# A planned five-queue attention and feed-forward kernel: transfers planned 1.3 times as long, new due times, first batch loaded in larger pieces

## The chip, the cores and the metric

The kernel runs on one core of a Trainium2 chip. The metric is the device time of one execution in microseconds (us), the median of several. Times of the kernel before drift by 1 to 3 us from chip to chip, so comparisons between runs go by the ratio to the kernel before, timed in the same rounds on the same chip.

## The reference, cut to what matters

```python
# batch 8, heads 12, sequence 448, head size 64; model width 768, hidden width 2048
q_n, k_n = rmsnorm(q, g_q), rmsnorm(k, g_k)
attn = softmax(q_n @ k_n.T / sqrt(64))
x = (attn @ v), heads side by side          # 8 * 448 rows of 768
h = x @ w_in                                # first layer
out = (h * erf(softplus(h))) @ w_out        # second layer
```

## The kernel before

The kernel records every operation with an engine, a planned cost, a due time and the tiles that it reads and writes. A small planner then simulates the five queues (P TensorE, V VectorE, A ScalarE, G GpSimd, S SyncE) and writes the operations out in the order in which its simulation started them. On the chip each queue runs in exactly that order. The planner is greedy: an engine that is free takes, of the operations that the simulation holds ready, the one with the earliest due time. When a transfer lands in the simulation decides which work counts as ready.

```python
    SEM = 0.06
    ...
        def dma_next():
            heads = [r[0] for r in rings.values() if r]
            ...
            cycle = sum(o.work[1] for o, _ in heads) / 16       # us per packet, 16 engines
            return dma_now + min(left[0] for _, left in heads) * cycle, cycle
```

`work` is the number of packets and the engine time of one; a landing comes `lat` after the last packet. Loads and due times, cut:

```python
    def add_unit(n, a_key):             # q and k of four heads of a later batch
        tg = (12 + 13 * u if b == 1 else BATCH * (b - 1) + 15 * u)
        ...  add("S", 0.59, tg - 15, dma_start(...), lat=1.7, work=(512, 0.038))
        ...  add("G", ..., tg, ... squares ...);  add("V", ..., tg, ... tensor_reduce ...)
    def add_norm(b, p):                 # scale k on GpSimd, q on VectorE: due 54 b + 9 p - 20
    def add_transposes(...):            # DMA transposes from SyncE: due t0 - 14
    def add_pe_transposes(p):           # batch 0: transposes on TensorE, k copied out by V, q by A
    def add_normalise(b, p, a_key):     # xT = o * r on VectorE: due -1e3 + t0
    def add_act_block(b, after):        # softplus, erf on ScalarE; g = h * sp on VectorE: due -1e4 + b
    def add_w_in(c, sync): ...          # 4 pieces of 1.5 MB f32, each waiting for the one before
    def add_w_out(c, sync): ...         # 8 pieces, all after pair 5 of batch 1
```

Batch 0 is loaded pair by pair (12 main transfers of 192 KB).

## Time and profile before

| | before |
|---|---|
| median of three | 518.85 us (518.63 to 518.98) |
| span of the profiled run | 517.3 us |
| busy: TensorE, ScalarE, VectorE, GpSimd | 465.3, 383.5, 329.6, 255.8 us |

TensorE's busy time overstates its use: it also contains idle products (put in to keep the clock up) and products at half clock. So this text counts products instead. The *lost time* of a stretch is its length less 0.190 us for each useful product of 448 columns and less 0.1625 us for each of 384 that the trace has in it, the rates of the gapless closing stream (18.24 us for 96, 36.41 us for 224). The small transposes of batch 0 and the idle products count as lost. A product that runs across a cut counts on both sides, so short stretches can sum to some 0.7 us less than one long stretch.

Two waits off TensorE matter later, from the view of waits of the kernel before (who waited, for whom: total us, times, longest; in profile lines PE is TensorE, PEld its weight load, DVE VectorE, ACT ScalarE, POOL GpSimd, SP SyncE, and a q marks the issue of a transfer):

```profile
POOL sq L284 <- DMA rq<-in_k_dram: 31.9, 13, 5.8
DVE qn L250 <- DMA qT<-qn: 25.3, 9, 9.3
```

GpSimd stands 31.9 us at squares whose data haven't landed, VectorE 25.3 us at scalings whose buffer a transposing transfer still reads. Both queues run in order, so all work behind them stands too.

### The profile page before, as it was taken

Reading aid. Unit: us, or ns where it says so; the run is one execution under the profiler, and the core shown is the slowest. Engines: PE = TensorE matmul, PEld = TensorE weight load, DVE = VectorE, ACT = ScalarE, POOL = GpSimd, SP = SyncE. Lnnn points to the kernel's source line nnn. Section 1 sums busy time; section 2 is a strip of 40 time slices with the busy share of each in tenths; the row PEclk is TensorE's granted clock in tenths of the full one; section 3 lists DMA queues with packets and bytes.
Section 4 is the critical chain, followed back from the end, with each engine's and each line's share of the span. In section 5 each row is a group of like instructions: output and inputs, shape, how many; then the busy total and the mean of one; then the engine's idle time right before and its main releaser. Section 6 shows DMA issues by size and latency. Waiting matters only on the chain.

```text
span 517.3 us, 7578 instructions
## 1 busy us (share of the span) xinstructions
PE 465.3 (90%) x2516; PEld 245.4 (47%) x2516; DVE 329.6 (64%) x493; ACT 383.5 (74%) x508; POOL 255.8 (49%) x411
## 2 busy tenths in 40 slices
PE   7867489958989898999889999999989999999997
PEld 3433235523445444554445444554545555555664
DVE  5866278668766886658654795649763873367721
ACT  3766648796868987799666987898877987995700
POOL 5559488784597257733674257743764050000000
PEclk9899979988999999999998999999999999999999
DMA  7976987895997056951886136962774041110122
GB/s 174 250 146 114 193 182 176 159 222 78 186 226 215 30 125 103 227 157 30 157 188 148 60 88 140 187 182 59 158 159 121 30 72 34 47 61 1 62 76 77
DMA packets 133415, 65.98 MB, mean 128 GB/s; under 512 B 84224, under 2 KB 133376, under 8 KB 133376
## 3 DMA queue, kind: packets, MB, share of 16 engines
q1 hardware_dynamic: 126320, 58.42, 49.7%
q0 software_dynamic: 5440, 6.29, 8.2%
q10 hardware_dynamic: 1616, 0.79, 0.6%
q8 instruction: 20, 0.33, 0.3%
q14 instruction: 19, 0.16, 0.1%
HBM read 45.61 MB, written 11.01 MB: 109 GB/s over the span
## 4 chain that ended last, share of the span: by engine, by line
PE 49%; DMA 16%; POOL 12%; DVE 10%; issue 6%; ACT 4%; SPq 2%; POOLq 0%; DVEq 0%
PE f L557 18%; PE f L508 16%; PE o L454 9%; PE s L432 6%; POOL sq L284 5%; DMA qT<-qn 5%; DMA rq<-in_k_dram 4%; DVE h L495 2%; DMA w_in_sb<-in_moe_w_in_dram 2%; DVE g L537 2%; DVE qn L250 2%; ACT e L438 2%; DMA sp<-in_k_dram 2%; POOL kn L258 1%; DVE xT L468 1%
## 5 line engine op out<-in xcount | busy, mean ns | idle before, releaser
L508 PE MATMUL f<-xT,w_in_sb 128*128 128x448 bf16 x768 | 165.3, 357 | 14.4 <-DVE h L495 12.1
L438 ACT ACTIVATE e<-s 128x896 bf16<-128x896 f32 x144 | 129.4, 913 | 19.6 <-PE s L432 10.9
L557 PE MATMUL f<-w_out_sb,g 128*128 128x384 bf16 x768 | 132.7, 327 | 1.2 <-DMA w_out_sb<-in_moe_w_out_dram 1.2
L508 PEld LDWEIGHTS <-w_in_sb 128*128 128x128 bf16 x768 | 75.8, 99 | 88.2 <-issue 21.7
L557 PEld LDWEIGHTS <-g 128*128 128x128 bf16 x768 | 75.4, 98 | 55.6 <-issue 4.6
L432 PE MATMUL s<-qT,kp 128*128 128x448 bf16 x336 | 96.1, 358 | 5.4 <-ACT e L438 2.4
L454 PE MATMUL o<-e,vm 128*128 128x448 bf16 x288 | 73.1, 359 | 21.0 <-DVE xT L468 16.5
L495 DVE COPY h<-f 128x448 f32<-128x448 f32 x109 | 67.3, 620 | 35.9 <-PE f L508 34.9
L495 DVE COPY ob<-f 128x384 f32<-128x384 f32 x53 | 29.5, 556 | 72.6 <-PE f L557 66.2
L258 POOL TENSOR_TENSOR kn<-rk,st 128x384 bf16<-128x384 f32 x42 | 38.7, 922 | 71.5 <-ACT st L291 62.9
L287 DVE TENSOR_REDUCE st<-sq 128x16 f32<-128x1024 f32 (+1 forms) x42 | 45.5, 1084 | 29.0 <-POOL sq L284 28.6
L537 DVE TENSOR_TENSOR g<-h,sp 128x768 bf16<-128x768 f32 x64 | 62.4, 1002 | 0.0
L462 ACT ACTIVATE r<-o 64x448 f32<-64x448 f32 x48 | 26.0, 541 | 45.5 <-PE o L454 45.1
L284 POOL TENSOR_TENSOR sq<-rq 128x1024 f32<-128x1024 f32 x21 | 40.1, 1911 | 38.7 <-DMA rq<-in_k_dram 31.9
L250 DVE TENSOR_TENSOR qn<-rq,st 128x512 bf16<-128x512 f32 x42 | 42.1, 1013 | 26.8 <-DMA qT<-qn 25.3
L522 ACT ACTIVATE sp<-h 128x1792 f32<-128x1792 f32 x32 | 52.0, 1687 | 5.4 <-DVE h L495 5.3
L454 PEld LDWEIGHTS <-vm 128*128 128x128 bf16 x288 | 28.2, 98 | 51.8 <-issue 24.9
L526 ACT ACTIVATE sp<-sp 128x1792 f32<-128x1792 f32 x32 | 52.6, 1690 | 0.1
L432 PEld LDWEIGHTS <-kp 128*128 128x128 bf16 x336 | 33.0, 99 | 36.8 <-issue 7.1
L315 POOL TENSOR_TENSOR qT<-qT,gcomb 128x448 bf16<-128x448 bf16 x42 | 41.4, 987 | 9.9 <-DMA qT<-qn 7.8
L468 DVE TENSOR_TENSOR xT<-o,r 64x448 bf16<-64x448 f32 x48 | 29.3, 611 | 10.0 <-ACT r L466 9.0
L408 POOL CAST vx<-vs 64x64 bf16<-64x64 f32 x96 | 25.9, 271 | 19.6 <-DMA vs<-in_v_dram 10.8
(64 smaller groups left out, 436.2 us busy)
## 6 DMA issues: line engine op xcount, KB each, us to landing
vl<-in_v_dram SPq DMA_DIRECT2D x48, 192.0 KB, 2.9
out_dram<-ob SPq DMA_DIRECT2D x48, 192.0 KB, 1.9
rq<-in_q_dram SPq DMA_DIRECT2D x21, 384.0 KB, 3.9
rk<-in_k_dram SPq DMA_DIRECT2D x21, 384.0 KB, 4.7
w_in_sb<-in_moe_w_in_dram POOLq DMA_DIRECT2D x4, 768.0 KB, 9.3
w_out_sb<-in_moe_w_out_dram POOLq DMA_DIRECT2D x8, 384.0 KB, 5.4
vs<-in_v_dram SPq DMA_DIRECT2D x16, 96.0 KB, 3.9
out_dram<-ob SPq DMA_DIRECT2D x16, 96.0 KB, 2.2
```

Of the source, the lines that this page charges most:

```text
L250: add(eng, cost, due, lambda: e.tensor_tensor(qn.rearrange("p g h d -> p h g d"), raw, w[:, :, :, None].to_broadcast((P, 2, 4, D)), op=ALU ...
L284: add("G", 0.0019 * ng * D, tg, lambda raw=raw, ng=ng: nc.gpsimd.tensor_tensor(sq[:, :ng], raw.rearrange("p h j d -> p (h j) d"), raw.rear ...
L287: add("V", 0.14 + ng * D / 960, tg, lambda ss=ss, g0=g0, ng=ng: nc.vector.tensor_reduce(ss[:, g0 : g0 + ng], sq[:, :ng], axis=AX.X, op=ALU ...
L432: add("P", 0.1887, t0 + s - 1, lambda st=st, i=i, c0=c0: nc.tensor.matmul(st[:, i, :S], kk[:, c0 : c0 + P], qq, start=True, stop=True), re ...
L438: add("A", 0.918, t0 + s, lambda e=e, st=st: nc.scalar.activation(e, st[:, :, :S], func=FN.Exp), reads=[("s", sl, 0), ("s", sl, 1), a_key] ...
L454: add("P", 0.1887, t0 + s + 0.5, lambda s=s, half=half, lhs=lhs, rhs=rhs: nc.tensor.matmul(o_ps[half][:, :S], lhs, rhs, start=(s == 0), st ...
L495: nc.vector.tensor_copy(dst, src)
L508: add("P", 0.1887, 1e4 + BATCH * (b + 1) + f, lambda f=f, kt=kt, fp=fp: nc.tensor.matmul(fp[:, :S], w_in_sb[:, kt, f * P : (f + 1) * P], x ...
L522: last = add("A", 1.665 + (1.283 if c == 0 else 0), -1e3, lambda c=c, ci=ci: nc.scalar.activation(sps[c], hs[ci], func=FN.Softplus), reads ...
L526: add("A", 1.665 + (1.283 if c == 0 else 0), -1e3, lambda c=c: nc.scalar.activation(sps[c], sps[c], func=FN.Erf), writes=[("sp", c, 1), "t ...
L537: add("V", 0.95, -1e4 + b, lambda h=h, s=s, gm=gm, a=a: nc.vector.tensor_tensor(gm[:, a], h[:, a, 0:384], s[:, a, 0:384], op=ALU.mult), re ...
L557: add("P", 0.1617, 1e4 + BATCH * (b + 2.5) + ti, lambda src=src, col=col, nt=nt, js=js, fp=fp: nc.tensor.matmul(fp[:, :JS], src[nt // 4][: ...
```

## The change

The intent is a plan that is nearer to what the chip does. The diff, cut to its core:

```diff
-    SEM = 0.06
+    SEM = 0.05
-            cycle = sum(o.work[1] for o, _ in heads) / 16
+            cycle = 1.3 * sum(o.work[1] for o, _ in heads) / 16
# due times (some 30 in all; the ones that the argument touches)
-        tg = (12 + 13 * u if b == 1 else BATCH * (b - 1) + 15 * u)
+        tg = 29.7 + 14.65 * u if b == 1 else BATCH * (b - 1) + 15.43 + 19.0 * u
-        add_norm_k("G", (0.86, 0.25), tg, ...            # tg = 54 b + 9 p - 20
+        add_norm_k("G", (0.86, 0.25), tg - 35.25, ...    # tg = 54 b + 9 p
-        add("G", 0.5, t0 - 5, ... vm cast
+        add("G", 0.5, t0 - 8.95, ... vm cast
-        add("V", 0.617, -1e3 + t0, ... xT
+        add("V", 0.617, -100 * 1e3 + t0, ... xT
-                    add("S", 0.59, BATCH * (b + 3), ... store of out
+                    add("S", 0.59, BATCH * (b + 0.68), ... store of out
# engines of batch 0
-        add("V", 1.08, t0 - 22, ... tensor_copy(kps[kp], tk)
+        add("A", {"V": 1.08, "A": 0.92}, t0 - 27.47, ... evac_to(mk, kps[kp], tk)
-        add("A", 0.545, t0 - 22, ... activation(qTs[m], tq, Copy, scale=gcomb)
+        add("VA", {"V": 0.617, "A": 0.545}, t0 - 27.47, gained, ...
# first loads: pairs 0 | 1 | 2 and 3 | 4 and 5
-        for p in range(NP):
-            main("S", p, 1, k)
-            main("A" if p < 3 else "S", p, 0, q)
+        for g, hh in enumerate((slice(0, 2), slice(2, 4), slice(4, 8), slice(8, H))):
+            for i, (e, src) in enumerate((("A" if g < 2 else "S", q), ("S", k))):
+                load(...)
# pacing of the weights
-    load, ends = add_w_in(0, [first]), []
+    load, ends = plan.writer[("q0", 1)], []
-            if b == 0 and p < NC - 1:
-                load = add_w_in(p + 1, [load, ends[-1]])
-            if b == 1 and p == NP - 1:          # all eight pieces of w_out
+            if b == 0 and 0 <= p - W_IN < NC:   # W_IN = 0
+                load = add_w_in(p - W_IN, [load, ends[-1]])
+            if b == 1 and p >= W_OUT:           # W_OUT = 3: pieces spread over pairs 3, 4, 5
```

The arithmetic of the kernel doesn't change. What changes is the order of the queues, the engine of twelve copies, the size of the first loads (eight of the twelve are joined into four), and the places of the weight loads.

## The prediction

> **What bounds the kernel now.** I first asked what the end of the run hangs on. The chain that ended last closes with two pieces:
>
> ```profile
> 459.32 18.24 PE f L508 x96
> 477.56 36.41 PE f L557 x224
> ```
>
> The columns are start, duration and what ran. From 459 us to the end TensorE streams without a gap. The two rows also give the rate of a full stream: 18.24 / 96 = 0.190 us for a product of 448 columns and 36.41 / 224 = 0.163 us for one of 384. The run therefore ends when TensorE has worked off a fixed amount, and only TensorE time lost earlier can be won back. The page counts 768 + 336 + 288 + 96 = 1488 useful products of 448 columns (first layer, scores, attention outputs) and 768 + 128 = 896 of 384 (second layer). That is 1488 x 0.190 + 896 x 0.163 = 283 + 146 = 429 us out of 517; some 88 us are lost.
>
> Next I read where, in the busy times of stretches that I chose by the digits of the page's slices (columns: stretch, its length, then PE, PEld, DVE, ACT, POOL busy with instruction counts, granted clock, DMA share, GB/s):
>
> ```profile
> 0.00:70.00 70.00, 47.47 (x249) 22.73 (x250) 39.54 (x76) 40.25 (x72) 43.57 (x93) 0.93 0.86 175
> 70.00:100.00 30.00, 29.21 (x152) 14.72 (x151) 24.36 (x35) 23.90 (x41) 26.77 (x43) 0.99 0.77 177
> 100.00:120.00 20.00, 12.30 (x55) 5.65 (x54) 12.98 (x18) 19.14 (x17) 12.99 (x17) 0.88 0.97 171
> 120.00:390.00 270.00, 252.63 (x1357) 133.05 (x1355) 188.64 (x265) 215.80 (x292) 160.10 (x236) 0.99 0.65 140
> 390.00:517.30 127.30, 123.65 (x709) 69.24 (x709) 64.07 (x102) 84.37 (x90) 12.41 (x25) 1.00 0.21 56
> ```
>
> The same stretches asked for single lines give the useful products: 117 (10 + 51 + 56; the other 132 are 66 idle products that keep the clock up and 66 small transposes) up to 70 us, so 70 - 22 = 48 us lost; 152 from 70 to 100 us, 1 us lost; 55 from 100 to 120 us, 20 - 10.5 = 9.5 us lost; 884 wide and 473 narrow from 120 to 390 us, 270 - 245 = 25 us lost; and 4 us in the rest, most of it the drain after the last product. So the first 120 us hold 57 of the 88 us. The first 70 us can't be emptied: batch 0 must pass attention before the first layer has rows to work on.
>
> What holds TensorE up in these stretches, from the view of waits (who waited, for whom, total, times, longest):
>
> ```profile
> PE o L454 <- DVE xT L468: 16.5, 13, 5.5
> PE f L508 <- DVE h L495: 12.1, 12, 3.9
> PE o L454 <- POOL vm L403: 4.1, 2, 2.9
> PE f L331 <- POOL g L258: 2.5, 1, 2.5
> ```
>
> None of these operations is slow; they stand behind others in the fixed order of their engine. Two places in the timeline show it (start, duration, engine, line, operation; in brackets the idle time before it):
>
> ```profile
> 26.61 1.89 POOL L284 TENSOR_TENSOR sq<-rq 128x1024 f32<-128x1024 f32 x1
> ...
> 30.21 0.96 POOL L403 CAST vm<-vl 128x384 bf16<-128x384 f32 x2
> ...
> 30.79 1.31 PE L454 MATMUL o<-e,vm 128*128 128x448 bf16 x6 [2.86 <-POOL vm L403]
> ```
>
> Here the squares of batch 1 and a weight load that waits 0.82 us for its predecessor stand ahead of the value cast that batch 0 needs at once.
>
> ```profile
> 55.68 5.61 SPq L309 DMA_TRANSPOSE kp<-kn  x1
> ...
> 61.39 1.21 SPq L312 DMA_TRANSPOSE qT<-qn  x1
> ...
> 64.77 1.09 DVE L250 TENSOR_TENSOR qn<-rq,st 128x512 bf16<-128x512 f32 x1 [9.26 <-DMA qT<-qn]
> 65.89 0.62 DVE L468 TENSOR_TENSOR xT<-o,r 64x448 bf16<-64x448 f32 x1
> ...
> 66.56 0.91 PE L454 MATMUL o<-e,vm 128*128 128x448 bf16 x2 [5.53 <-DVE xT L468]
> ```
>
> VectorE stands 9.26 us at a query scaling of batch 1, whose buffer a transposing transfer has yet to read; the transfer stands in SyncE's queue behind another. The normalisation that frees the PSUM of batch 0 stands behind the scaling, and TensorE behind that. At 100 to 120 us it is the same: the square waited 2.8 us for its load, the reduction on VectorE 3.5 us for the square, and the first layer 3.9 and 3.1 us for evacuations on VectorE.
>
> **What the Trainium skill says.** "DMA: Bandwidth & Descriptors", section "Issuing engines are not separate DMA queues", says that transfers from all issuing engines run on the same 16 DMA engines and interleave, so several issuers save only issue time. The trace agrees: the share is 0.98 and 1.01 at 10 to 30 us, with sync, scalar and gpsimd issues in flight together. So fewer, larger first loads save issues (0.37 to 0.84 us each) but hardly bytes per us. The same page's "Bandwidth" gives 341 GB/s for 1 MB; here the best of the 40 slices has 250. "TensorE: Matmul & The Clock Gate", Part 1, says that an idle array falls to half clock for some 3.4 us. The trace agrees: after the gap at 61 to 66.6 us weight loads come 0.37 us apart, not 0.19, and the clock in 100 to 120 us is 0.88, so a long gap costs more than itself. "GPSIMD Engine Reference", section "Specifications", has GpSimd's SBUF interface shared with VectorE's two-input operations; L250 takes 0.69 us when undisturbed and 1.01 in the mean here.
>
> **The change, part by part.** It adds and removes almost no work; it re-sorts five queues.
>
> *Transfers 1.3 times as long.* The plan's unit of 896 KB has 512 x 0.038 x 2 + 256 x 0.018 x 2 = 48.1, over 16 engines 3.0 us plus 1.7, which is about 305 GB/s. The trace lands the large loads in 3.9 and 4.7 us and moves 175 GB/s in the busy first part. So the old plan puts users of a load ahead of work that is really ready sooner. A factor of 1.3 (235 GB/s) is nearer. It answers the waits on queries and squares above.
>
> *Due times.* Preparation of the next batch's unit goes from 12 + 13u to 29.7 + 14.65u for batch 1 and 15 to 23 later for others, so the square at 26.6 us should no longer pass ahead of the cast at 30.2 us. The cast's own due goes from -5 to -8.95. Normalisation (-1e5) now outranks the products of the activation block (-1e4), which before outranked it. Stores of the output become due 2.3 batches earlier; VectorE waited 6.2 us for those buffers.
>
> By stage, taking half of what the waits name where the order is the cause. Up to 70 us: casts 4.1 + transposes 2.5 + normalisation 7.2 (of the 16.5, the share before 75 us) = 13.8 us, plus some 12 products at the slow clock, 12 x 0.18 = 2 us; half of 16 is 8 us. From 100 to 120 us: 9.5 us lost, and I take 4 back, since ScalarE is busy 19.1 of 20 us there with the softplus and erf block and stays so. From 120 to 390 us: normalisation 9.3 and stores' knock-on; I take 3.
>
> *First batch.* Main loads go from 12 to 8, 4 x 0.47 = 2 us of issue saved on SyncE; the load of v's last rows (vs), for which the first cast waits 8.6 us, was issued at 12.7 us. Bytes ahead of it are the same: 1 us won. But pairs 2 and 3 now wait for one common load.
>
> *What it costs.* Six key evacuations move from VectorE (0.62 us each) to ScalarE (0.92, estimated from the exponent of the same size, 0.913) and six query evacuations (0.63) may leave it: +5.5 - 3.8 = +1.7 us on ScalarE, which is on the way in batch 0. First-layer weights start a pair later (17.8 us to about 20.5, after pair 0); four transfers of 9.3 us, one after another, then end near 63 us rather than 61. Together I charge 3 us.
>
> Sum: -8 - 4 - 3 - 1 + 3 = -13 us, which is 506.
>
> **Rivals.** (1) The first 70 us are bound by bytes: DMA share 0.86 there and 1.01 at the worst. Then the re-sorted order only moves the wait from casts to loads, and only the later 7 us are won: 512, within 2%. Against it speaks that the share falls to 0.58 at 40 to 50 us, in the midst of the stall. (2) The late preparation makes batch 1 start late: its squares and scalings fall into 60 to 100 us, where GpSimd is already busy 26.8 of 30 us, and TensorE waits for kp and qT. With second-layer weights now starting at pair 3 of batch 1 instead of pair 5, GpSimd also gets up to five issues of 0.76 us there. That gives 515 to 525. (3) The order fits so much better that stage 1 nears ScalarE's bound (37.2 us of work in the 56 us from 10 to 66): 12 us won there and 8 later, 498.
>
> **Range and chances.** The lines are 508.5 (2% faster) and 529. The three rivals spread 498 to 520; I take 506, and 494 to 517 for eight in ten. As the dues look fitted to a model and not to round numbers, and the wait they address is seen in the trace, faster has 0.61; same 0.35; slower 0.04.
>
> **What would show it.** Right: in the new profile the first first-layer stream starts before 65 us instead of 70.9; the 9.26 and 5.53 us waits are gone; the wait of attention outputs for the normalisation falls from 16.5 to under 9 us; the clock at 60 to 70 us is near 1; the last stream has the same length and starts some 13 us sooner. Wrong: kp or qT waits of TensorE at 60 to 100 us (rival 2), or a DMA share near 1 right through 10 to 60 us with the first-layer stream still near 70 (rival 1). The sum fails if new head-of-line waits appear after 120 us, since there the dues changed everywhere.

## The result, and the profile after

The changed kernel took 493.61 us in the median (492.1 to 494.1, 4 runs), beside 518.91 us (518.63 to 520.23) for the kernel before: ratio 0.9503, 95% interval 0.9476 to 0.953. The prediction was 506 us with a range of 494 to 517; the gain of some 25 us is twice the predicted one and just outside the range.

The end of the chain of waits of the changed kernel (start, duration, what):

```profile
432.09 18.16 PE f L515 x96
450.25 36.41 PE f L564 x224
```

The closing stream is as long as before (18.16 and 36.41 against 18.24 and 36.41 us) and starts 27 us sooner. TensorE's rate didn't change; time lost before 432 us was won back. (Line numbers moved: L515 is the first layer, L564 the second, L445 scores, L467 attention outputs.) The busy times of the same stretches (columns as in the prediction):

```profile
0.00:70.00 70.00, 56.55 (x300) 28.05 (x301) 47.86 (x86) 53.70 (x90) 50.71 (x106) 0.95 1.00 192
70.00:100.00 30.00, 28.81 (x150) 14.37 (x149) 22.31 (x30) 25.10 (x35) 25.75 (x38) 1.00 1.17 223
100.00:120.00 20.00, 13.23 (x60) 6.19 (x59) 14.72 (x20) 17.12 (x21) 11.99 (x16) 0.83 0.73 140
120.00:390.00 270.00, 263.38 (x1452) 141.67 (x1451) 195.86 (x278) 236.12 (x309) 161.10 (x242) 1.00 0.64 140
390.00:490.30 100.30, 96.65 (x561) 54.57 (x558) 47.28 (x76) 57.75 (x62) 5.05 (x13) 1.00 0.19 51
```

Asked for single lines, these stretches hold 168, 150, 60, 908 and 209 useful wide products, and 544 and 352 narrow ones in the last two. That gives:

| stretch | lost before, us | lost after, us | won | predicted |
|---|---|---|---|---|
| 0 to 70 | 47.8 | 38.1 | 9.7 | 6 (8 + 1 - 3) |
| 70 to 100 | 1.1 | 1.5 | -0.4 | 0 |
| 100 to 120 | 9.6 | 8.6 | 1.0 | 4 |
| 120 to 390 | 25.2 | 9.1 | 16.1 | 3 |
| 390 to the end | 4.2 | 3.4 | 0.8 | 0 |

The sum is 27 us, which is the difference of the spans, 517.3 - 490.3. (The rows up to 120 us sum to 58.5 and 48.2; counted as one stretch, as in the tables below, they are 59.2 and 48.8, for the cuts.) The big surprise is the fourth row. The waits of TensorE that answer to those of the prediction:

```profile
PE f L515 <- ACT h L332: 7.4, 3, 6.8
PE o L467 <- DVE xT L481: 3.0, 4, 1.4
PE f L515 <- DVE h L330: 2.5, 4, 1.1
```

The wait for the normalisation fell from 16.5 to 3.0 us and the one for VectorE's evacuations from 12.1 to 2.5; a new one of 6.8 us stands at the top. And the two waits off TensorE:

```profile
POOL sq L285 <- DMA rq<-in_k_dram: 10.5, 9, 1.8
DVE qn L251 <- DMA qT<-qn: 4.6, 6, 1.7
```

GpSimd's stop for loads fell from 31.9 to 10.5 us, VectorE's stop for transposes from 25.3 to 4.6, the longest from 9.3 to 1.7. The transfers themselves became no faster: the steady loads of k (384 KB) land in a median of 4.7 us before and 4.6 after, pieces of w_in in 9.3 and 9.2.

The new 6.8 us, from the timeline of the changed kernel:

```profile
106.38 0.51 ACT L332 COPY h<-f 128x448 f32<-128x448 f32 x1
...
106.94 5.31 PE L515 MATMUL f<-xT,w_in_sb 128*128 128x448 bf16 x17 [6.77 <-ACT h L332]
```

The copy out of PSUM writes h, which has five buffers of four tiles; the fifth is full, and the first is free only when batch 0's products g = h * sp have read it. These need the erf block of ScalarE, which needs the softplus block. By the trace's single instructions the products that read the first tile had ended at 105.47 us; the copy then stood until 106.38 behind the third erf in ScalarE's queue. In the second batch TensorE has no second-layer work yet to fill this time (its first product of that kind comes after 120 us). So most of this wait hangs on ScalarE's chain and on h's five buffers, and about 0.9 us of it on the order. A sixth buffer would test this; no run has it, so it stays argued from the timeline and the code.

### The profile page after: what moved, and what is told of

It is laid out like the page before. It is cut to its first block, busy times and chain, and to the rows that moved or that the text cites. A ratio compares the mean times of both kernels' runs of the same rounds, so it can differ in the third digit from the quotient of the medians. Undisturbed runs are those within 1.5% of the kernel's fastest.

```text
span 490.3 us, 7518 instructions
## 1 busy us (share of the span) xinstructions
PE 458.6 (94%) x2516; PEld 244.9 (50%) x2516; DVE 328.0 (67%) x487; ACT 389.8 (79%) x514; POOL 254.6 (52%) x411
## 4 chain that ended last, share of the span: by engine, by line
PE 56%; DMA 16%; POOL 8%; DVE 8%; ACT 6%; issue 4%; SPq 2%; POOLq 0%; DVEq 0%
PE f L564 24%; PE f L515 16%; PE o L467 8%; PE s L445 7%; DMA qT<-qn 4%; DMA rq<-in_k_dram 3%; POOL sq L285 3%; DMA w_in_sb<-in_moe_w_in_dram 2%; DVE st L288 2%; ACT sp L533 2%; DVE qn L251 2%; DMA w_out_sb<-in_moe_w_out_dram 1%; ACT sp L529 1%; DMA rk<-in_k_dram 1%; DMA sp<-in_q_dram 1%
## 5 line engine op out<-in xcount | busy, mean ns | idle before, releaser
L515 PE MATMUL f<-xT,w_in_sb 128*128 128x448 bf16 x768 | 164.0, 355 | 10.3 <-ACT h L332 7.4
L564 PE MATMUL f<-w_out_sb,g 128*128 128x384 bf16 x768 | 129.2, 326 | 0.3 <-DVE ob L330 0.3
L515 PEld LDWEIGHTS <-w_in_sb 128*128 128x128 bf16 x768 | 75.5, 98 | 82.8 <-issue 15.4
L445 PE MATMUL s<-qT,kp 128*128 128x448 bf16 x336 | 94.8, 357 | 7.2 <-ACT e L451 2.9
L564 PEld LDWEIGHTS <-g 128*128 128x128 bf16 x768 | 75.1, 98 | 52.5 <-issue 1.9
L330 DVE COPY h<-f 128x448 f32<-128x448 f32 x106 | 65.4, 621 | 34.9 <-PE f L515 34.2
L467 PE MATMUL o<-e,vm 128*128 128x448 bf16 x288 | 71.2, 352 | 4.2 <-DVE xT L481 3.0
L416 POOL CAST vm<-vl 128x384 bf16<-128x384 f32 x48 | 29.6, 618 | 80.0 <-PE o L467 78.9
L544 DVE TENSOR_TENSOR g<-h,sp 128x768 bf16<-128x768 f32 x64 | 59.9, 967 | 0.0
L251 DVE TENSOR_TENSOR qn<-rq,st 128x512 bf16<-128x512 f32 x42 | 45.1, 1101 | 9.3 <-DMA qT<-qn 4.6
L445 PEld LDWEIGHTS <-kp 128*128 128x128 bf16 x336 | 32.8, 98 | 36.3 <-issue 6.7
L285 POOL TENSOR_TENSOR sq<-rq 128x1024 f32<-128x1024 f32 x21 | 39.8, 1893 | 13.8 <-DMA rq<-in_k_dram 10.5
L467 PEld LDWEIGHTS <-vm 128*128 128x128 bf16 x288 | 27.8, 97 | 34.2 <-issue 8.8
L259 POOL TENSOR_TENSOR kn<-rk,st 128x384 bf16<-128x384 f32 x42 | 40.5, 964 | 7.1 <-DMA kp<-kn 4.1
L481 DVE TENSOR_TENSOR xT<-o,r 64x448 bf16<-64x448 f32 x48 | 29.3, 611 | 17.9 <-ACT r L479 17.6
```

The costliest lines, as they stand in the source:

```text
L251: add(eng, cost, due, lambda: e.tensor_tensor(qn.rearrange("p g h d -> p h g d"), raw, w[:, :, :, None].to_broadcast((P, 2, 4, D)), op=ALU ...
L285: add("G", 0.0019 * ng * D, tg, lambda raw=raw, ng=ng: nc.gpsimd.tensor_tensor(sq[:, :ng], raw.rearrange("p h j d -> p (h j) d"), raw.rear ...
L330: nc.vector.tensor_copy(dst, src)
L445: add("P", 0.1887, t0 + s - 1.17, lambda st=st, i=i, c0=c0: nc.tensor.matmul(st[:, i, :S], kk[:, c0 : c0 + P], qq, start=True, stop=True), ...
L467: add("P", 0.1887, t0 + s + 0.43, lambda s=s, half=half, lhs=lhs, rhs=rhs: nc.tensor.matmul(o_ps[half][:, :S], lhs, rhs, start=(s == 0), s ...
L515: add("P", 0.1887, 1e4 + BATCH * (b + 1) + f, lambda f=f, kt=kt, fp=fp: nc.tensor.matmul(fp[:, :S], w_in_sb[:, kt, f * P : (f + 1) * P], x ...
```

## The experiments

Eighteen kernels ran, all correct, each with 3 rounds (4 runs) against the kernel before on the same chip. Beside the ratio the tables give the lost time of TensorE up to 120 us and from 120 to 390 us, counted as above in each run's profile.

### Which part carries the gain

**t_alone**: the kernel before, with one line changed.

```diff
-            cycle = sum(o.work[1] for o, _ in heads) / 16
+            cycle = 1.3 * sum(o.work[1] for o, _ in heads) / 16
```

> The kernel before with only the factor 1.3 on the planned transfers. Theory A (the due times carry the gain: VectorE's and GpSimd's order is what held TensorE up): within 6 us of before, 513 to 522 us, and TensorE's wait for the normalisation stays above 10 us. Theory B (the plan's belief in too fast transfers is the cause): at least half of the 25 us come, 500 to 507 us, and that wait falls below 8 us.

Measured: 508.95 us, ratio 0.9771 (0.9709 to 0.9833). The wait for the normalisation fell from 16.5 to 4.3 us. The time lies between the two theories' figures, with 0.0229 of the changed kernel's 0.0497, a little under half of the gain; the wait is where theory B put it. By the 2% rule of the record the verdict is unclear, as the interval reaches 0.9833; that there is a gain at all is clear.

**no_t**: the changed kernel without that line.

```diff
-            cycle = 1.3 * sum(o.work[1] for o, _ in heads) / 16
+            cycle = sum(o.work[1] for o, _ in heads) / 16
```

> The changed kernel with the transfers planned at their old length (factor 1.0). Theory A: at most 6 us lost, 493 to 500 us. Theory B: more than half of the gain lost, 506 us or more, with loads' users early in VectorE's and GpSimd's order again (GpSimd's wait for the rq loads from 10 back to some 30 us).

Measured: 514.89 us, ratio 0.9903 (0.9851 to 0.9956). Theory A is out: without the factor nearly the whole gain is gone although every due time is new. GpSimd's wait for loads rose to 19.4 us (less than the 30 expected). The timeline of no_t shows the kind of stop that the prediction found in the kernel before, at another place:

```profile
79.74 1.26 SPq L313 DMA_TRANSPOSE qT<-qn  x1
...
89.13 0.69 DVE L251 TENSOR_TENSOR qn<-rq,st 128x512 bf16<-128x512 f32 x1 [8.06 <-DMA qT<-qn]
...
91.66 0.53 PE L515 MATMUL f<-xT,w_in_sb 128*128 128x448 bf16 x1 [6.97 <-DVE h L330]
```

VectorE stands 8.06 us at a scaling that waits for a transpose, the evacuation of the first layer stands behind it in the queue, and TensorE 6.97 us behind that. The transfer, issued at 79.74 us, landed 9.3 us later, while a piece of w_out and other transfers were under way. The planner is plain Python and can be run off the chip: in no_t's plan the same transfer lands 4.0 us after its issue, and the scaling starts 0.1 us after that. So the plan put the scaling right behind a landing that came 5 us later than planned.

**dues_alone**: the kernel before with all new due times (but old factor, loads, pacing, engines).

```diff
-        tg = (12 + 13 * u if b == 1 else BATCH * (b - 1) + 15 * u)
+        tg = 29.7 + 14.65 * u if b == 1 else BATCH * (b - 1) + 15.43 + 19.0 * u
# ... and every other due time of the change
```

> The kernel before with all new due times, but transfers at the old length, old first loads, old pacing of the weights and old engines. Theory A: most of the gain, 496 to 503 us. Theory B: less than 10 us, 509 us or more. A third theory, that first loads and pacing carry it by the first 70 us, also says 509 or more.

Measured: 515.97 us, ratio 0.9934 (0.9866 to 1.0002), which can't be told from no gain.

**no_dues**: the changed kernel with all due times old.

```diff
-        tg = 29.7 + 14.65 * u if b == 1 else BATCH * (b - 1) + 15.43 + 19.0 * u
+        tg = (12 + 13 * u if b == 1 else BATCH * (b - 1) + 15 * u)
# ... and every other due time of the change
```

> The changed kernel with all due times as before; factor 1.3, first loads, pacing and engines stay new. Theory A: most of the gain lost, 508 to 518 us, and TensorE's wait for the normalisation back above 10 us. Theory B: at least half kept, 506 us or less.

Measured: 498.51 us, ratio 0.9585 (0.9534 to 0.9636): four fifths of the gain stay. The wait for the normalisation was 3.7 us with the old due of -1e3, so it isn't the new due that ended it.

**no_loads**: batch 0 loaded pair by pair again.

```diff
-        for g, hh in enumerate((slice(0, 2), slice(2, 4), slice(4, 8), slice(8, H))):
-            ...
+        for p in range(NP):
+            main("S", p, 1, k)
+            main("A" if p < 3 else "S", p, 0, q)
```

> The changed kernel with the first batch loaded pair by pair again (12 main transfers). My sum had 1 us for the larger loads: 493 to 497 us. Rival (the first loads carry the part of the gain that neither factor nor dues explain, some 10 us): 500 us or more, lost before 70 us.

Measured: 501.09 us, ratio 0.9638 (0.9578 to 0.9698). As large as the rival said, but not lost where it said: up to 60 us this kernel loses even less (34.7 against 37.6 us; the first-layer products start at 52 us, in the changed kernel at 55.8). The loss is at 60 to 120 us (19.0 against 10.8) and in the later part (12.1 against 9.1). Why larger first loads help there isn't settled.

**no_pace**: the weights at their old places.

```diff
-            if b == 0 and 0 <= p - W_IN < NC:
-                load = add_w_in(p - W_IN, [load, ends[-1]])
-            if b == 1 and p >= W_OUT:
+            if b == 0 and p < NC - 1:
+                load = add_w_in(p + 1, [load, ends[-1]])
+            if b == 1 and p == NP - 1:
```

> The changed kernel with the weights loaded at the old places (w_in one pair earlier, all of w_out after pair 5 of batch 1). If the pacing is worth nothing: 491 to 496 us. If it carries the unexplained 10 us: 500 us or more, with the loss between 60 and 160 us.

Measured: 503.83 us, ratio 0.968 (0.9629 to 0.9731). The pacing counts, but 7 of the some 10 us are lost up to 60 us, not after. From the timeline of no_pace:

```profile
15.76 0.87 POOL L495 DMA_DIRECT2D w_in_sb<-in_moe_w_in_dram  x1 [6.94 <-DVE g L250]
16.92 0.63 POOL L420 CAST vx<-vs 64x64 bf16<-64x64 f32 x1 [0.30 <-DMA vs<-in_v_dram]
21.43 1.28 POOL L258 TENSOR_TENSOR g<-sp,s 128x384 bf16<-128x384 f32 x1 [3.87 <-ACT s L391]
...
26.90 0.50 POOL L415 CAST vm<-vl 128x384 bf16<-128x384 f32 x1
...
29.67 0.89 PE L466 MATMUL o<-em,vx 128*128 128x448 bf16 x2
```

and of the changed kernel:

```profile
17.87 0.95 POOL L416 CAST vm<-vl 128x384 bf16<-128x384 f32 x2
...
21.85 0.54 PE L467 MATMUL o<-em,vx 128*128 128x448 bf16 x2
```

The PE lines are the last attention outputs of pair 0. With the first weights issued at 15.8 us they start at 29.7 us, with the weights issued at 22.9 us already at 21.9. The trace tells what delays them. In both runs v's main rows land in 5.4 to 5.5 us, by 18.4 us in no_pace and by 17.6 in the changed kernel, so neither the weights' bytes nor GpSimd's stand at the issue makes v late. But no_pace's order has the casts of v behind key scalings that wait for ScalarE (3.87 us), so the first ran at 26.9 us and not at 17.9. Run off the chip, no_pace's planner has v land 15 us after its issue, beside the weights' transfer (the changed kernel's, without it, 10). So here the plan held a landing to be much later than it was; that this is why the casts stand so late is argued.

**no_engines**: the copies of batch 0 where they were.

```diff
-        add("A", {"V": 1.08, "A": 0.92}, t0 - 27.47, lambda: evac_to(mk, kps[kp], tk[:, 0 : 7 * P]), ...
+        add("V", 1.08, t0 - 27.47, lambda: nc.vector.tensor_copy(kps[kp], tk[:, 0 : 7 * P]), ...
-        add("VA", {"V": 0.617, "A": 0.545}, t0 - 27.47, gained, ...
+        add("A", 0.545, t0 - 27.47, lambda: nc.scalar.activation(qTs[m][:, :S], tq[:, :S], func=FN.Copy, scale=gcomb), ...
```

> The changed kernel with the key evacuation of batch 0 on VectorE and the gained query copy on ScalarE, as before. My sum charged 1.7 us of ScalarE's time to the new places, so it would be equal or 1 to 2 us faster: 490 to 495 us. Rival (the freed VectorE is what lets batch 0 through): 498 us or more.

Measured: 498.21 us, ratio 0.9588 (0.9485 to 0.9692). There is no sign that the new places cost anything. The median says that they are worth some 4 us, but the interval overlaps that of the changed kernel (0.9476 to 0.953), so a gain isn't shown either. The difference in lost time is mostly after 120 us (12.7 us lost there, not 9.1), where the twelve copies are long done; if it is real, it is an effect on the order that follows, not ScalarE's or VectorE's time.

**t_loads_pace**: the kernel before with factor, first loads and pacing.

```diff
# the hunks of t_alone, and the new first loads and pacing; dues, engines and SEM old
```

> The kernel before with factor 1.3, the grouped first loads and the new pacing of the weights; old dues, old engines, old semaphore wait. If these three carry the change: 496 to 502 us, some 55 us lost up to 120 us as in the kernel without dues (52) and below 17 us after. If the new engines of batch 0 are needed too: 503 us or more.

Measured: 502.67 us, ratio 0.9634 (0.9579 to 0.9689), a bit short of the first expectation.

In one ladder, where rows with a + have the parts of the row above too:

| kernel | ratio | lost to 120 us | lost 120 to 390 us |
|---|---|---|---|
| before | 1 | 59.2 | 25.2 |
| dues alone | 0.9934 | 59.6 | 21.5 |
| factor 1.3 alone (t_alone) | 0.9771 | 58.4 | 16.5 |
| + first loads and pacing (t_loads_pace) | 0.9634 | 54.1 | 12.5 |
| + engines and SEM (no_dues) | 0.9585 | 52.7 | 11.9 |
| + dues (the changed kernel) | 0.9503 | 48.8 | 9.1 |
| the changed kernel less the factor (no_t) | 0.9903 | 60.0 | 19.5 |

The factor is worth 2.3% first and 4.0% last; the dues are worth 0.7% first (an interval that includes nothing at all) and 0.8% last. The intervals of t_loads_pace and no_dues overlap, so the step of engines and SEM isn't told apart from none. The factor alone wins its 9 us in the later part. The first 120 us improve only when pacing and loads come to it, and not without the factor.

### Is it the factor, or luck with the order?

Any edit of the plan reshuffles hundreds of operations. Two edits without a reason of their own measure that noise.

**sem06** and **before_sem05**: the plan's wait per semaphore exchanged, alone.

```diff
# sem06, from the changed kernel
-    SEM = 0.05
+    SEM = 0.06
# before_sem05, from the kernel before
-    SEM = 0.06
+    SEM = 0.05
```

> The changed kernel with the plan's wait per semaphore 0.06 again instead of 0.05, nothing else: a second change of the order without a reason of its own, beside factor 1.25, which cost 5 us. If the changed kernel is one lucky order among its neighbours: 496 to 502 us. If factor 1.25 lost for a reason of its own: within 2 us, 491 to 496 us.

> The kernel before with the plan's wait 0.05: the same test on the other side. If the kernel before is an ordinary order: anything from 514 to 524 us. If it was an unlucky one that any new order improves: below 512 us, and then the 10 us of factor 1.3 alone would be no proof of the factor.

Measured: sem06 493.06 us, ratio 0.9443 (0.9374 to 0.9512); before_sem05 521.75 us, ratio 1.0004 (0.9947 to 1.006). Neither start is a lucky or unlucky order in this direction. sem06 is not told apart from the changed kernel, whose interval meets its own. The edit does reorder: run off the chip, the planner of sem06 moves 338 of 2516 TensorE instructions against the changed kernel (all that don't keep their order), that of factor 1.25 moves 434. before_sem05 shows one thing more:

```profile
POOL sq L284 <- DMA rq<-in_k_dram: 30.9, 14, 4.0
DVE qn L250 <- DMA qT<-qn: 7.4, 6, 2.7
```

VectorE's wait for transposes fell from 25.3 to 7.4 us, its longest from 9.3 to 2.7, and nothing was won. So that wait by itself is not what the kernel before loses its time to.

**t115, t125, t14, t16**: other factors in the changed kernel.

```diff
-            cycle = 1.3 * sum(o.work[1] for o, _ in heads) / 16
+            cycle = 1.15 * sum(o.work[1] for o, _ in heads) / 16      # 1.25, 1.4, 1.6
```

> The changed kernel with factor 1.15. On a smooth slope it lies between 1.0 and 1.25: 500 to 510 us. If the orders are lottery tickets, it may be anything, also below 499 or above 514 us.

> The changed kernel with factor 1.25 in place of 1.3: a measure of how far any change of the order moves the time by itself. If the order is robust: within 3 us, 490 to 497 us. If the numbers were fitted to this very order: 498 us or more, which would put every single-part figure of this study under the doubt of several us.

> The changed kernel with factor 1.4. On a smooth slope it lies between 1.3 and 1.6: 495 to 504 us, with the loss before 120 us. If lottery: anything, also above 508 us. If it is below 491 us, 1.3 is not the best setting.

> The changed kernel with factor 1.6. If what counts is only that the plan doesn't believe in too fast transfers: as factor 1.25, 495 to 503 us. If 1.3 is near the true length and more is as wrong as less: 505 us or more, with the loss in the first 120 us, where transfers are planned too late.

| factor | median us | ratio (95% interval) | lost to 120 us | lost 120 to 390 us |
|---|---|---|---|---|
| 1.0 (no_t) | 514.89 | 0.9903 (0.9851 to 0.9956) | 60.0 | 19.5 |
| 1.15 | 503.24 | 0.9693 (0.964 to 0.9745) | 54.8 | 15.0 |
| 1.25 | 499.4 | 0.9592 (0.9545 to 0.9638) | 54.3 | 11.4 |
| 1.3 (changed) | 493.61 | 0.9503 (0.9476 to 0.953) | 48.8 | 9.1 |
| 1.4 | 498.28 | 0.9605 (0.9535 to 0.9675) | 52.5 | 12.3 |
| 1.6 | 511.11 | 0.9794 (0.9743 to 0.9846) | 61.9 | 14.5 |

Factor 1.25 came out at 499.4 us, which by my own expectation puts every single-part figure under the doubt of several us; the steps of 4 to 5 us (dues, engines) stand under it. For the factor itself sem06 and the other values lessen the doubt: the time has one valley with its bottom at 1.3 among the values tried, and by the ratios 1.0 lies some 21 us and 1.6 some 15 us above it. More caution isn't better: at 1.6 the first 120 us are as bad as at 1.0, though GpSimd's wait for loads (9.7 us) and VectorE's for transposes (3.1) are the smallest of the series. (At 1.4 the loss is not before 120 us alone, as I expected, but almost half of it after.) That the bottom lies just at 1.3 may partly come from due times that were chosen with it; the ladder's first step doesn't depend on these.

### Which transfers, and is it length or delay?

**f_weights, f_transposes, f_loads**: the factor for one kind of transfer only.

```diff
-            cycle = 1.3 * sum(o.work[1] for o, _ in heads) / 16
# f_weights
+            cycle = sum((1.3 if o.eng == "G" else 1.0) * o.work[1] for o, _ in heads) / 16
# f_transposes: if o.work[1] == 0.02
# f_loads: if o.eng != "G" and o.work[1] in (0.038, 0.018)
```

> The changed kernel with 1.3 only for the weights (gpsimd queue), all else 1.0. If the weights, by sharing the engines, are what delays the transposes: gain kept up to 120 us, total 493 to 500 us. If the steady traffic of q, k and v is: as factor 1.0, 508 to 516 us, with some 23 us lost after 120 us, where weights have long landed.

> 1.3 only for the DMA transposes (planned 0.56 us of engine time for k, 0.32 for q, each plus 1.7, while the trace lands them in 3.8 and 2.9). If the misjudged transposes alone block VectorE: 493 to 502 us and VectorE's longest wait for one under 3 us. If they only suffer from the loads ahead of them: 508 us or more.

> 1.3 only for the loads of q, k and v from the sync and scalar queues. If these are the cause: the late loss stays below 16 us and the total is 494 to 503 us. Else 506 us or more.

**t_lat**: factor 1.0, each landing planned 1 us later.

```diff
-                gap = 0.0 if e == "P" == u.eng else o.lat + self.SEM
+                gap = 0.0 if e == "P" == u.eng else o.lat + (1.0 if o.work else 0.0) + self.SEM
```

> Factor 1.0, but every landing planned 1 us later. If any later landing serves as a margin: 493 to 502 us. If the length per byte counts, since it adds up in a queue behind others: 505 us or more, with a stop of VectorE over 5 us where weights and loads meet before 120 us.

| kernel | median us | ratio (95% interval) | lost to 120 us | lost 120 to 390 us | VectorE's longest wait for a transpose |
|---|---|---|---|---|---|
| no_t | 514.89 | 0.9903 (0.9851 to 0.9956) | 60.0 | 19.5 | 8.1 |
| f_weights | 511.52 | 0.9819 (0.9765 to 0.9873) | 58.6 | 16.9 | 2.7 |
| f_transposes | 509.96 | 0.9771 (0.9738 to 0.9805) | 60.0 | 14.2 | 2.4 |
| f_loads | 504.62 | 0.9671 (0.9637 to 0.9705) | 56.2 | 13.1 | 3.9 |
| t_lat | 506.17 | 0.9684 (0.9633 to 0.9735) | 57.3 | 14.2 | 2.3 |
| all at 1.3 | 493.61 | 0.9503 (0.9476 to 0.953) | 48.8 | 9.1 | 1.7 |

No single kind is the cause. Each of them ends the 8 us stop (none left over 4 us), yet by the ratios none brings more than 0.023 of the 0.040 between no_t and the changed kernel; the loads of q, k and v bring most. The interval of f_weights overlaps that of no_t, so a gain of the weights isn't shown. f_transposes ended the stop and still lost 60.0 us up to 120 us, as no_t did: its total lies where I put it if the transposes only suffer from the loads ahead of them. A fixed microsecond also brings about half, so part of the effect is simply a later landing, and half a gain needs no exact model. f_weights landed in the range of my second case (508 to 516 us), but with 16.9 us lost after 120 us and not some 23. For f_loads the late loss came as the cause would have it and the total just above the range; t_lat lost what length per byte asked for, but without the stop of over 5 us.

Two versions were not run: all at 1.3 but the weights, and the stores of the output alone at 1.3. No experiment gave a version that is clearly better than the changed kernel.

## Why the prediction was wrong, point by point

**The bound was right.** The last stream kept its length and started 27 us sooner, as the prediction asked for; only lost TensorE time was won.

**Up to 70 us, predicted 8 + 1 - 3: right in sum, wrong in its parts.** 9.7 us were won. The wait for the normalisation in this stretch fell from 7.2 to 1.4 us, the cast's from 4.1 to nothing (0.8 us are left in the whole run, later). But the late start of the first-layer weights, which I charged as part of 3 us of cost, is a gain: undoing the pacing gives 503.8 us in place of 493.6, with 44.6 instead of 37.6 us lost up to 60 us. The weights were also issued later than I reckoned (22.9 us, not 20.5; the last piece at 58.1, landed at 68.8 and not near 63). The engines that I charged too showed no cost. The joined loads save three issues on SyncE and one on ScalarE, not four on SyncE, so 1.4 us and not 2. And my sign that first-layer work would start before 65 us instead of 70.9 was misread: ten such products already ran from 57.7 us in the kernel before; 70.9 was the restart after the stop.

**100 to 120 us, predicted 4: wrong.** One us was won. I saw that ScalarE was full there and still took 4 back. The profile after puts the remaining 6.8 us on ScalarE's softplus and erf blocks and the buffers of h.

**120 to 390 us, predicted "normalisation 9.3 and stores' knock-on; I take 3": this is the step that failed.** 16.1 us were won. I had 25 us lost there in my own reckoning, and in the same stretch GpSimd waiting 21 us for loads and VectorE 12 us for transposes, and I left these out because they are not TensorE's waits. I also gave the factor no term. The factor alone takes this stretch from 25.2 to 16.5 us, and TensorE's wait for the normalisation in it from 9.3 to 3.6; that is shown. That it works through those two waits is argued from the timelines, and their totals don't measure it: in the same stretch dues_alone has them at 17.2 and 3.7 us and loses 21.5, t_alone at 18.3 and 10.8 and loses 16.5.

**What I thought the cause was.** I wrote that 1.3 "answers the waits on queries and squares" and gave it no figure of its own; the sum went by due times. The runs say: factor 2.3% alone and 4.0% last, dues 0.7 and 0.8%. My comparison of the plan's rates with the trace pointed the right way. Done for each landing it would have said more. The formula for a transfer that is alone doesn't do it, since in the plan the queues share the engines. So the planners of three kernels were run off the chip. From issue to landing, medians in us, as planned and as traced:

| transfer | no_t (1.0): plan, trace | changed (1.3): plan, trace | t16 (1.6): plan, trace |
|---|---|---|---|
| load of q, 384 KB | 2.9, 3.7 | 3.4, 3.7 | 4.0, 4.1 |
| load of k, 384 KB | 3.5, 4.6 | 4.3, 4.6 | 5.2, 4.7 |
| load of v | 2.3, 2.9 | 3.0, 3.0 | 4.7, 2.9 |
| transpose of k | 2.3, 3.4 | 3.9, 3.8 | 4.4, 3.4 |
| transpose of q | 2.0, 2.8 | 3.1, 2.9 | 4.0, 2.8 |
| piece of w_in | 9.3, 8.1 | 11.0, 9.2 | 13.0, 7.7 |
| piece of w_out | 5.5, 5.8 | 6.3, 5.7 | 7.4, 5.1 |

At 1.3 the plan agrees with the trace for SyncE's loads and transposes; at 1.0 it has all of these too early, at 1.6 most too late. The weights were about right or too late already at 1.0, and 1.3 makes them worse. That fits the runs: f_weights alone shows no clear gain, f_loads and f_transposes do. It is an agreement of medians, not a proof that this agreement is what the time follows.

**The rivals.** Rival 1 (bytes bind the first 70 us) fell: the DMA share rose from 0.86 to 1.00 there and the time was won all the same. Rival 2 (late preparation hits 60 to 100 us) didn't happen in the changed kernel (1.5 us lost at 70 to 100) but is what no_t shows, new dues with the old factor: 8.06 us of VectorE and 6.97 of TensorE in that very stretch. Rival 3's 498 us came nearest, by luck: it had 12 us up to 70 us (9.7 were won) and 8 later, where 17 were, for a reason that it didn't name.

**The half clock.** The prediction said that a long gap costs more than itself. At 60 to 70 us the granted clock was 0.70 before and is 1.00 after, as its sign asked. At 120 to 390 us TensorE's idle time fell from 270 - 252.6 = 17.4 to 270 - 263.4 = 6.6 us, which is 10.8 of the 16.1 us won. The other 5.3 us are busy time in which products came at less than the full rate before. The mean granted clock rose from 0.99 to 1.00 there; 1% of 270 us is 2.7 us, an estimate of what the clock had of it. The rest isn't explained.

## What to carry to other kernels

When a planner fixes the order of in-order queues, check its assumed landing times against the trace, transfer kind by transfer kind, before tuning priorities: here that was worth 2.3 to 4.0%, and some thirty new priorities 0.7 to 0.8%. Compare what the planner simulates with all queues at work, not its formula for one transfer. To size such a change, count the bound engine's lost time by stretch, and look also at the other queues' waits for transfers, but don't add them up: a meaningless edit took 18 us off VectorE's and won nothing. And measure an edit without meaning (here 0.01 us of a semaphore wait, which reordered the queues and left the time) before reading a few microseconds of a reshuffled order as an effect.

## What the Trainium skill lacked or had wrong

- "DMA: Bandwidth & Descriptors", section "Bandwidth", gives rates of single transfers by size, 341 GB/s for 1 MB. In this mix of loads, casting weights and transposes the best of 40 slices of the profile has 250 GB/s before and 256 after, and the steady loads of 384 KB land in 3.7 to 4.7 us, those of the first batch in 6.2 to 6.5. It has no figure for landings in mixed traffic, which is what a planner needs.
- The same page, section "DMA Transpose (X-bar)", gives constraints but no time from issue to landing beside other transfers. (The page has a bandwidth for them elsewhere.) Here it is 3.4 to 3.8 us in the median for k's tile and 2.7 to 2.9 for q's, and one in no_t took 9.3 us and held VectorE's queue for 8.06.
- "Perfetto Trace Analysis", section "Identifying the Most-Contended Engine", says to optimise the engine with the highest occupancy first; its next section, "Optimization Strategy", says to find what its gaps wait for. Neither says to look at the waits of the less busy in-order queues, which here moved with the gain in the changed kernel (GpSimd's and VectorE's waits for transfers from 31.9 and 25.3 to 10.5 and 4.6 us), nor that such waits can fall without a gain (VectorE's to 7.4 us in before_sem05).
